# Two query loads and one store moved to ScalarE's DMA queue, and a shorter sum in the last group

## The chip, the cores and the metric

The kernel runs on one core of one Trainium2 chip. A core has five engines that run their own instruction lists in order and wait for each other by semaphores: TensorE (PE; its weight loads are listed as PEld), VectorE (DVE), ScalarE (ACT), GpSimd (POOL) and SyncE (SP). SyncE only issues DMAs here; ScalarE can issue them too, from its own queue. Both queues feed the same 16 DMA engines. In the profile SyncE's row of DMA rings is q1 and ScalarE's is q10. The metric is device microseconds for one execution of the whole program.

## The reference, cut to what matters

The first part is a linear attention with decay. For batch 4, 8 heads, sequence 768 and head size 64, it takes q, k, v and a decay `lam` for each head:

```
intra = (qb @ kb.T * Dmask) @ vb                # inside a block
inter = (qb * lam_pow) @ kv_state               # from earlier blocks
out   = intra + inter
kv_state = lam_block * kv_state + (kb * rev_pow).T @ vb
```

The second part is a feed-forward layer on the 3072 x 512 result: `h = x @ w_in`, `g = h * sigmoid(h)`, output `g @ w_out`, with `w_in` 512 x 2048 and `w_out` 2048 x 512. All inputs and outputs are float32.

## The kernel before, in words

The kernel works on 24 chunks of 128 tokens, all heads at once, in bf16 on TensorE. The feed-forward layer takes the tokens in 12 groups of 256, that is two chunks each. The order on every engine is the order in which the Python code issues the instructions; no scheduler changes it.

**The start.** Line 75 has ScalarE issue the load of `lam` (4 KB, read into 128 partitions). Lines 119 to 131 make the decay tables `lam_fwd` and `lam_bwd` from it, with a table load on ScalarE ahead and another one behind (line 872). The first two pairs of chunks (chunks 0 and 1, chunks 2 and 3) are loaded by the list `LOADS` (line 21), which is walked at line 834 by way of `load_pair` (line 219). A word like `K01` is the letter of the input, the first chunk of the pair (0) and the half of the heads (1). Each word is one DMA of 256 KB, in runs of 512 bytes, and all twelve are issued by SyncE, in the order of the list. In the text Q00 is the query load of the first half of the heads of the first pair, and so on.

What then happens to these tiles is written out by hand in `ORDER` (line 23): `kc` and `qc` scale and cast a half (the first one, `kc:0,0`, is only cast) on VectorE, GpSimd or ScalarE; `tk` and `tq` transpose it on TensorE; `kt` and `qt` copy the transposes out of PSUM; `s` makes the scores, `m` masks them on VectorE, `d` makes the state, `i` and `o` the two parts of the attention, `x` copies the result out, `w` casts a part of `w_in`, `u` and `g` are the first products of the feed-forward layer. `z` puts matmuls on a tile of zeros between them (line 874). On TensorE the start of this list stands as `tk:0,0`, two zero matmuls of 512 columns, `tq:0,0`, four zero matmuls of 256 columns, `tk:0,1`, scores. Weight pieces are loaded by SyncE behind the twelve words, each as soon as a buffer comes free; later pairs of chunks follow them.

Each DMA takes one of eight semaphores in turn (`lam` the first, then the words of the list), and a DMA that uses a semaphore again waits for the one that used it before: Q20 for `lam`, K21 for K00, Q21 for Q00, V20 for K01, V21 for Q01.

**The middle.** Around 35 to 41 us the pair of chunks 4 and 5 is prepared: GpSimd makes eight products (lines 364 and 365) from the loaded queries and keys, TensorE transposes them (lines 399 and 413) between matmuls of the second feed-forward product of the first two groups (line 664).

**The end of a group.** From group 2 on, the product with `w_out` for a group of 256 tokens is done as one step of Strassen's scheme, with seven products instead of eight (`seven`, line 741). `product(g, n, ...)` (line 730) runs product n as eight matmuls into `place[n]` in PSUM. The result is four quarters of 128 tokens by 256 columns in the tile `ob`: quarter 0 is the first tokens and first columns, 1 the first tokens and last columns, 2 and 3 the same for the last tokens. In the last group the seven products come in the order 3, 4, 1, 6, 2, 5, 7, each followed by a small function; product 2 adds into the tile of product 4, and product 5 into that of product 3. The tile `m` holds the sum of products 3, 4 and 1. `last_2` copies quarter 2 out of PSUM on ScalarE and stores it, then makes quarter 3 on VectorE in two steps; `last_5` copies quarter 1 on ScalarE, stores it, and starts quarter 0; `last_7` adds product 7 and stores quarter 0. The four stores of 128 KB each are issued by SyncE (`put`, line 758).

Of the kernel before, what the change touches and what calls it, by code (L numbers as in the profile page):

```python
# [7 lines left out]
F32 = mybir.dt.float32  # L8
BF16 = mybir.dt.bfloat16
AF = mybir.ActivationFunctionType  # L10
AL = mybir.AluOpType

BLK = 128
# [4 lines left out]

NPET = 6

LOADS = "K00 Q00 K01 Q01 V00 V01 K20 Q20 K21 Q21 V20 V21"

ORDER = """
wl kc:0,0,D,u z:24,210 qc:0,0,D tk:0,0,o z:2,512 tq:0,0,att kc:0,1,D,s kt:0,0,A qc:0,1,D z:4 qt:0,0,A tk:0,1,h s:0,0,h,o
# [12 lines left out]
def kernel(  # L37
# [10 lines left out]
    nc = tc.nc  # L48
    B, H, S, D = q.shape
    assert (B, H, S, D) == (4, 8, 768, 64)  # L50
    NB = S // BLK
# [9 lines left out]
    const = ctx.enter_context(tc.tile_pool(name="const", bufs=1))  # L61
# [11 lines left out]
    lam_sb = const.tile([128, H], F32)  # L73
    lam_bc_ap = bass.AP(tensor=lam.tensor, offset=lam.offset, ap=[[0, 128]] + list(lam.ap))
    nc.scalar.dma_start(out=lam_sb, in_=lam_bc_ap)

# [8 lines left out]
        out=ident, in_=ident, compare_op=AL.not_equal, fill=1.0,  # L87
# [4 lines left out]
    for r in range(2):  # L92
        for i in range(2):
            rows = slice(64 * i, 64 * i + 64)
            nc.gpsimd.affine_select(
                out=mask_p[rows, r], in_=mask_p[rows, r], compare_op=AL.is_ge, fill=0.0,
# [5 lines left out]
        out=mask, in_=mask, compare_op=AL.is_ge, fill=0.0,  # L102
# [8 lines left out]
    for i in range(NKV):  # L111
# [14 lines left out]
        op=AL.mult,  # L126
# [11 lines left out]

    wtmp = {}
    pad2 = const.tile([128, 288], mybir.dt.uint8, name="pad2")  # L140

    pairs = [const.tile([128, 2 * H * D], F32, name=f"pair{i}") for i in range(6)]
    npair = iter(range(99))

    def next_pair():
        return pairs[next(npair) % 6]

    def w_piece(which, i, a, b):
        if which == "in":
# [4 lines left out]
    def load_w(which, *pieces):  # L154
        for i in pieces:
            if which == "in" and i > 5:
                tag = "kf" if i == 6 else "vf"
                wtmp[which, i] = []
                for a in range(2):
                    ko, f = w_piece(which, i, a, a + 1)  # L160
                    t = io.tile([128, 1, 512], F32, name=tag, tag=tag, bufs=6)
                    nc.sync.dma_start(out=t, in_=w_in_r[:, ko, f])
                    wtmp[which, i].append(t)
                continue
            ko, f = w_piece(which, i, 0, 2)
            t = next_pair().rearrange("p (k f) -> p k f", k=2)
            nc.sync.dma_start(out=t, in_=(w_in_r if which == "in" else w_out_r)[:, ko, f])
            wtmp[which, i] = t
# [18 lines left out]
    def bank(tag):  # L187
        if tag != "o":
            return {"tag": tag, "bufs": NBUF[tag]}
        otag[0] = 1 - otag[0]  # L190
        return {"tag": f"o{otag[0]}", "bufs": 1}
# [23 lines left out]
    def load_q(c):  # L215

        load_pair(q, c, rawq)

    def load_pair(src, c, dst, parts=((0, H),)):
        b, blk = divmod(c, NB)  # L220
        for lo, hi in parts:
            if c not in dst:
                dst[c] = next_pair().rearrange("p (h r d) -> p h r d", h=H, r=2)
            nc.sync.dma_start(out=dst[c][:, lo:hi].rearrange("p h r d -> p h (r d)"),  # L224
                              in_=src[b, lo:hi, blk * BLK:(blk + 2) * BLK, :].rearrange("h (p r) d -> p h (r d)", r=2))

    rawq, rawk, vraw = {}, {}, {}

    def load_1(src, c, tag, bufs, e=None):
        b, blk = divmod(c, NB)  # L230
# [443 lines left out]
    HALF = DM // 2  # L674
# [25 lines left out]
    lo, hi = slice(0, 128), slice(128, 256)  # L700
# [20 lines left out]
    def g_diff(g, j):  # L721

        one = quad(g, j)
        d = sum_tile(g, "gd", j // 2, 128)[:, j % 2]
        a, b = (hi, lo) if j < 2 else (lo, hi)
        nc.vector.tensor_tensor(d, one[:, :, a], one[:, :, b], op=AL.subtract)  # L726
        for u in range(4):
            gs[g, 6 if j < 2 else 7, 4 * (j % 2) + u] = d[:, u, :]

    def product(g, n, dst, start):  # L730

        tick()
        for k in range(K2):
            if n in (3, 4):
                lhsT = gt[g, k][:, 0:128] if n == 3 else gt[g, K2 + k][:, 128:256]
            else:
                lhsT = gs[g, n, k]
            rhs = w_block(n, k, (0, 0))[:, 0, :] if n == 2 else w_block(n, k, (1, 1))[:, 0, :] if n == 5 else wsum[n, k]
            nc.tensor.matmul(dst, lhsT=lhsT, rhs=rhs, start=(start and k == 0), stop=(k == K2 - 1), skip_group_check=True)  # L739

    def seven(g):

        last = g == len(GROUPS) - 1
        if last:
            tags = ("o0", 1), ("o1", 1), ("att", 3), ("att", 3), ("h", 2)
            tiles = [psum.tile([128, HALF], F32, name="o_last", tag=t, bufs=b, padded_shape=[128, 512]) for t, b in tags]
            place = dict(zip((3, 4, 1, 6, 7), tiles))
            place[5], place[2] = place[3], place[4]
        else:
            o = [psum.tile([128, 2, HALF], F32, name="o_ps", **bank("o")) for _ in range(2)]  # L750
            place = {3: o[0][:, 0, :], 4: o[0][:, 1, :], 5: o[0][:, 0, :], 2: o[0][:, 1, :],
                     1: o[1][:, 0, :], 7: o[1][:, 0, :], 6: o[1][:, 1, :]}
        ob = pairs[g] if g < 6 else opool.tile([128, 4 * HALF], F32, name="ob", tag="ob")
        quarters = ob.rearrange("p (a n) -> p a n", a=4)
        m = work.tile([128, HALF], F32, name="msum", tag="msum", bufs=2)
        r0 = gstart[g]

        def put(rows, cols, src):
            dst = out[r0 + BLK * rows:r0 + BLK * rows + BLK, cols[0]:cols[1]]
            if last:  # L760
                nc.sync.dma_start(out=dst, in_=src)
            elif g < 6:
                held.append((dst, src))
            else:
                stores.append([0, dst, src])

        def after_3():
            nc.scalar.activation(m, place[3], AF.Copy)

        def after_4():  # L770
            if not last:
                after_3()
            nc.vector.tensor_tensor(m, m, place[4], op=AL.add)
            if g > 3:
                g_diff(g, 3)

        def after_sums():
            for j in (2, 3)[g - 2:]:
                g_diff(g, j)

        def after_1():
            nc.vector.tensor_tensor(m, m, place[1], op=AL.add)

        def after_2():
            nc.scalar.activation(quarters[:, 1:3, :], o[0], AF.Copy)
            nc.vector.tensor_tensor(quarters[:, 0::3, :], m[:, None, :].to_broadcast([128, 2, HALF]), o[0], op=AL.subtract)

        def after_7():
            nc.vector.tensor_tensor(quarters[:, 0::3, :], quarters[:, 0::3, :], o[1], op=AL.add)
            for t in range(2):  # L790
                put(t, (0, DM), ob[:, DM * t:DM * t + DM])

        def quarter(a):

            side = (0, 1, 0, 1)[a]
            put(a // 2, (HALF * side, HALF * side + HALF), quarters[:, a, :])

        def last_2():
            nc.scalar.activation(quarters[:, 2, :], place[2], AF.Copy)
            quarter(2)  # L800
            nc.vector.tensor_tensor(quarters[:, 3, :], m, quarters[:, 2, :], op=AL.subtract)
            nc.vector.tensor_tensor(quarters[:, 3, :], quarters[:, 3, :], place[6], op=AL.add)
            quarter(3)

        def last_5():
            nc.scalar.activation(quarters[:, 1, :], place[5], AF.Copy)
            quarter(1)
            nc.vector.tensor_tensor(quarters[:, 0, :], m, quarters[:, 1, :], op=AL.subtract)

        def last_7():  # L810
            nc.vector.tensor_tensor(quarters[:, 0, :], quarters[:, 0, :], place[7], op=AL.add)
            quarter(0)

        if last:
            order = [(3, True, after_3), (4, True, after_4), (1, True, after_1), (6, True, None),
                     (2, False, last_2), (5, False, last_5), (7, True, last_7)]
        else:
            order = [(3, True, None), (4, False, after_4), (1, True, after_sums if g < 4 else None), (6, False, after_1),
                     (5, False, None), (2, False, after_2), (7, True, after_7)]

        def step(n, start, after):
            def run():
                product(g, n, place[n], start)
                if after:
                    after()
            return run

        return [step(*x) for x in order]
# [1 line left out]
    nch = [n // BLK for n in GROUPS]  # L830
    cst = [sum(nch[:g]) for g in range(len(GROUPS))]


    for word in LOADS.split():
        a = int(word[2])
        src, dst = {"Q": (q, rawq), "K": (k, rawk), "V": (v, vraw)}[word[0]]
        load_pair(src, int(word[1]), dst, ((4 * a, 4 * a + 4),))

    later = [("in", i, {f"{t}:{b},{a}" for a in range(2)}) for i, (b, t) in enumerate((b, t) for b in (0, 2) for t in ("kc", "qc", "vc"))]
    later += [("in", 6, set()), ("in", 7, set())] + [("out", i, {f"w:{n},{a}" for a in range(2)}) for n, i in enumerate((0, 1, 4, 5, 2, 3))]  # L840
# [48 lines left out]
    for word in ORDER.split():  # L889
        name, _, args = word.partition(":")  # L890
# [88 lines left out]
    for g in range(2, len(GROUPS) - 1):  # L979
        c, d, a, b = range(2 * g + 2, 2 * g + 6)  # L980
# [79 lines left out]
```

## Time and profile before

| what | us |
|---|---|
| three runs | 196.33, 197.43, 198.35 (median 197.43) |
| the profiled execution | 197.22 |
| its span, from the first to the last instruction | 195.4 |
| TensorE busy | 189.0 |
| VectorE busy | 132.7 |
| ScalarE busy | 101.6 |
| GpSimd busy | 72.7 |

A line of the timeline has the start in us, the duration in us, the engine, the line of the kernel, the operation, what is written and read, and how often it was repeated; brackets give the idle time of the engine before it and what ended that. "SPq" and "ACTq" are the issues of DMAs by SyncE and ScalarE, whose duration is that of the issue and not of the transfer. In the slices each digit is the busy share of one slice in tenths. A queue's line has its packets, its MB, and its time as a share of 16 DMA engines. The trace also records when each of the 16 DMA engines has completed its part of a load; a load has landed when all 16 have. The granted TensorE clock was 0.999 over the span.

### The profile page before, as it was taken

The page shows a single profiled execution, that of the slowest core. Times are in us where ns is not written, and L with a number is a line of the kernel's source. Part 1 is how long each engine was busy: PE and PEld are TensorE (multiplying, and loading weights), DVE is VectorE, ACT ScalarE, POOL GpSimd, SP SyncE. Part 2 cuts the span into 40 slices and gives each one's busy share as a digit, 9 for nine tenths or more (in the row PEclk, how much of TensorE's full clock was granted, in tenths as well). Part 3 has the DMA queues.
Part 4 walks back from the last instruction along what each step waited for, and adds up shares of the span by engine and source line. Part 5 has one row for each costly group of instructions (what it writes and reads, how often), then busy time and mean ns, then how long its engine had stood idle before and what let it go on. Part 6 is the DMA issues. An engine that isn't in the chain of part 4 may idle for free.

```text
span 195.4 us, 6705 instructions
## 1 busy us (share of the span) xinstructions
PE 189.0 (97%) x2859; PEld 154.1 (79%) x2864; DVE 132.7 (68%) x253; ACT 101.6 (52%) x191; POOL 72.7 (37%) x126
## 2 busy tenths in 40 slices
PE   7889999999999999999999999999999999999993
PEld 6568544546888888888888888888888888888882
DVE  1797267978999476875755865975875846754443
ACT  3875974153853844662662652652752752733621
POOL 5240000928937526834704851850940200200000
PEclk9999999999999999999999999999999999999999
DMA  3999999999979799949879499798899840200203
GB/s 93 333 354 406 404 403 334 234 274 280 177 163 285 99 172 245 205 84 229 154 164 236 92 221 158 166 235 168 190 375 220 251 186 3 107 3 0 111 0 107
DMA packets 95581, 38.71 MB, mean 198 GB/s; under 512 B 80960, under 2 KB 88640, under 8 KB 95552
## 3 DMA queue, kind: packets, MB, share of 16 engines
q1 hardware_dynamic: 90208, 36.97, 77.1%
q10 hardware_dynamic: 5344, 1.32, 3.1%
q8 instruction: 22, 0.36, 0.8%
q14 instruction: 7, 0.06, 0.1%
HBM read 27.27 MB, written 6.29 MB: 172 GB/s over the span
## 4 chain that ended last, share of the span: by engine, by line
PE 89%; SPq 3%; DMA 2%; DVE 2%; issue 1%; POOL 1%; ACT 0%; ACTq 0%; DVEq 0%; POOLq 0%
PE h_ps L619 38%; PE o_ps L739 29%; PE o_ps L664 6%; PE h_ps L858 5%; PE op L540 4%; SPq L224 3%; DMA pair<-in_q_dram 2%; PE o_last L739 2%; PE sp L540 2%; PE kv_ps L540 1%; DVE ss L560 1%; POOL vp L253 1%; POOL qb L253 1%; PE op L313 0%; PE op L323 0%
## 5 line engine op out<-in xcount | busy, mean ns | idle before, releaser
L619 PE MATMUL h_ps<-xt,w_in_bf 128*128 128x256 bf16 x672 | 76.2, 272 | 0.0
L619 PEld LDWEIGHTS <-w_in_bf 128*128 128x128 bf16 x672 | 65.4, 98 | 8.9 <-issue 0.3
L631 ACT ACTIVATE g<-h_ps 128x512 bf16<-128x512 f32 x84 | 49.9, 597 | 33.9 <-PE h_ps L619 32.6
L180 POOL CAST kvs<-total 128x256 bf16<-128x256 f32 x26 | 10.4, 407 | 35.8 <-DVE total L575 26.6
L726 DVE TENSOR_TENSOR gd<-g 128x512 bf16<-128x512 bf16 x40 | 20.5, 523 | 3.8 <-ACT g L631 3.8
L364 POOL TENSOR_TENSOR qb<-qf,lam_fwd 128x256 bf16<-128x256 f32 x18 | 12.5, 692 | 20.6 <-DMA qf<-in_q_dram 13.1
L712 DVE TENSOR_TENSOR gc<-g 128x512 bf16<-128x512 bf16 x20 | 10.3, 517 | 14.1 <-ACT g L631 14.1
L178 ACT ACTIVATE xt<-op 128x256 bf16<-128x256 f32 (+1 forms) x18 | 8.1, 484 | 22.5 <-PE op L540 22.5
L739 PE MATMUL o_ps<-w_out_bf,gb 128*128 128x256 bf16 x144 | 18.8, 273 | 0.0
L739 PE MATMUL o_ps<-wsum,gd 128*128 128x256 bf16 x144 | 18.7, 273 | 0.0
L182 DVE CAST xt<-op 128x256 bf16<-128x256 f32 (+1 forms) x16 | 8.3, 541 | 14.9 <-PE op L540 13.9
L739 PE MATMUL o_ps<-wsum,g 128*128 128x256 bf16 x144 | 17.2, 273 | 0.0
L739 PEld LDWEIGHTS <-gd 128*128 128x128 bf16 x160 | 15.7, 98 | 1.8
L739 PEld LDWEIGHTS <-g 128*128 128x128 bf16 x160 | 15.7, 98 | 1.8
L714 DVE TENSOR_TENSOR gb<-g 128x1024 bf16<-128x1024 bf16 x20 | 17.0, 850 | 0.0
L739 PEld LDWEIGHTS <-gb 128*128 128x128 bf16 x160 | 14.9, 98 | 2.0
L364 POOL TENSOR_TENSOR kb<-kf,lam_bwd 128x256 bf16<-128x256 f32 x20 | 14.3, 713 | 5.2 <-DMA kf<-in_k_dram 5.2
L575 DVE TENSOR_TENSOR total<-total,kv_ps 128x256 f32<-128x256 f32 x33 | 13.8, 418 | 2.4 <-ACT total L178 0.2
L664 PE MATMUL o_ps<-w_out_bf,g 128*128 128x512 bf16 x60 | 14.3, 379 | 0.5 <-issue 0.3
L365 POOL TENSOR_TENSOR kb<-kf,lam_bwd 128x256 bf16<-128x256 f32 x20 | 14.3, 714 | 0.0
L365 POOL TENSOR_TENSOR qb<-qf,lam_fwd 128x256 bf16<-128x256 f32 x18 | 13.6, 754 | 0.0
L560 DVE TENSOR_TENSOR ss<-sp,mask 128x512 bf16<-128x512 f32 x20 | 12.8, 681 | 0.2 <-PE sp L540 0.2
(107 smaller groups left out, 251.0 us busy)
## 6 DMA issues: line engine op xcount, KB each, us to landing
vf<-in_v_dram SPq DMA_DIRECT2D x20, 256.0 KB, 4.2
kf<-in_k_dram SPq DMA_DIRECT2D x18, 256.0 KB, 5.0
pair<-in_moe_w_out_dram SPq DMA_DIRECT2D x8, 512.0 KB, 7.8
qf<-in_q_dram SPq DMA_DIRECT2D x15, 256.0 KB, 4.4
pair<-in_moe_w_in_dram SPq DMA_DIRECT2D x6, 512.0 KB, 7.2
out_dram<-pair SPq DMA_DIRECT2D x12, 256.0 KB, 3.8
out_dram<-ob SPq DMA_DIRECT2D x10, 256.0 KB, 3.2
pair<-in_k_dram SPq DMA_DIRECT2D x4, 256.0 KB, 4.5
```

What stands on the lines that cost most here:

```text
L180: nc.gpsimd.tensor_copy(dst, src)
L364: eng.tensor_tensor(dst[:, 0::2], src[:, 0::2, ::-1, :], by[:, 0::2, ::-1, :], op=AL.mult)
L365: eng.tensor_tensor(dst[:, 1::2], src[:, 1::2], by[:, 1::2], op=AL.mult)
L540: ins = nc.tensor.matmul(dst, lhsT=lhsT, rhs=rhs, start=start, stop=True, skip_group_check=True)
L560: nc.vector.tensor_tensor(ss, sp.rearrange("k w p q -> k (w p) q"), mask64[:, None, :].to_broadcast([128, len(scores) * NP, D]), op=AL.mult)
L575: nc.vector.tensor_tensor(total[b], old, place(c, h), op=AL.add)
L619: nc.tensor.matmul(hps[g, i][:, a:a + 256], lhsT=w_in_bf[:, ko, m * 128:(m + 1) * 128], rhs=xt[g][:, ko, :], start=(ko == 0 and u == 0), s ...
L631: nc.scalar.activation(gg.rearrange("p u n -> p (u n)"), hps[g, i], AF.Silu)
L664: nc.tensor.matmul(o, lhsT=gt[g, ko][:, mt * BLK:(mt + 1) * BLK], rhs=w_out_bf[:, ko, :], start=(ko == 0), stop=(ko == KO_OUT - 1))
L714: nc.vector.tensor_tensor(both, low, one, op=AL.add)
L726: nc.vector.tensor_tensor(d, one[:, :, a], one[:, :, b], op=AL.subtract)
L739: nc.tensor.matmul(dst, lhsT=lhsT, rhs=rhs, start=(start and k == 0), stop=(k == K2 - 1), skip_group_check=True)
```

## The change

The words `Q00` and `Q01` of the list become `Q00A` and `Q01A`: ScalarE issues these two loads, behind the load of `lam` and ahead of its first table load. The loop over the list is moved up to directly behind the load of `lam`, with `load_pair` and the buffers that it uses. SyncE issues the other ten words in their order. The semaphores are handed out as before.

In the last group, a new step behind product 6 adds `place[6]` to `m` into quarter 3; behind product 2 only the subtraction of quarter 2 is left to do for quarter 3. Behind product 5, quarter 0 is now started by VectorE straight from PSUM, `m - place[5]`, instead of from the copy that ScalarE made of it; ScalarE's copy of the same tile for quarter 1 comes behind it in the program, and waits for it. The store of quarter 1 is issued by ScalarE.

```diff
-LOADS = "K00 Q00 K01 Q01 V00 V01 K20 Q20 K21 Q21 V20 V21"
+LOADS = "K00 Q00A K01 Q01A V00 V01 K20 Q20 K21 Q21 V20 V21"
...
     nc.scalar.dma_start(out=lam_sb, in_=lam_bc_ap)
+
+    pairs = [const.tile([128, 2 * H * D], F32, name=f"pair{i}") for i in range(6)]
...
+    def load_pair(src, c, dst, parts=((0, H),), e=None):
...
+            (e or nc.sync).dma_start(out=dst[c][:, lo:hi].rearrange("p h r d -> p h (r d)"),
+                              in_=src[b, lo:hi, blk * BLK:(blk + 2) * BLK, :].rearrange("h (p r) d -> p h (r d)", r=2))
+
+    for word in LOADS.split():
+        a = int(word[2])
+        src, dst = {"Q": (q, rawq), "K": (k, rawk), "V": (v, vraw)}[word[0]]
+        load_pair(src, int(word[1]), dst, ((4 * a, 4 * a + 4),), nc.scalar if word[3:] else None)
...
-        def put(rows, cols, src):
+        def put(rows, cols, src, e=None):
             dst = out[r0 + BLK * rows:r0 + BLK * rows + BLK, cols[0]:cols[1]]
             if last:
-                nc.sync.dma_start(out=dst, in_=src)
+                (e or nc.sync).dma_start(out=dst, in_=src)
...
+        def last_6():
+            nc.vector.tensor_tensor(quarters[:, 3, :], m, place[6], op=AL.add)
 
         def last_2():
             nc.scalar.activation(quarters[:, 2, :], place[2], AF.Copy)
             quarter(2)
-            nc.vector.tensor_tensor(quarters[:, 3, :], m, quarters[:, 2, :], op=AL.subtract)
-            nc.vector.tensor_tensor(quarters[:, 3, :], quarters[:, 3, :], place[6], op=AL.add)
+            nc.vector.tensor_tensor(quarters[:, 3, :], quarters[:, 3, :], quarters[:, 2, :], op=AL.subtract)
             quarter(3)
 
         def last_5():
+            nc.vector.tensor_tensor(quarters[:, 0, :], m, place[5], op=AL.subtract)
             nc.scalar.activation(quarters[:, 1, :], place[5], AF.Copy)
-            quarter(1)
-            nc.vector.tensor_tensor(quarters[:, 0, :], m, quarters[:, 1, :], op=AL.subtract)
+            quarter(1, nc.scalar)
...
-            order = [(3, True, after_3), (4, True, after_4), (1, True, after_1), (6, True, None),
+            order = [(3, True, after_3), (4, True, after_4), (1, True, after_1), (6, True, last_6),
                      (2, False, last_2), (5, False, last_5), (7, True, last_7)]
```

More of the change, by code (lines that the diff above doesn't have):

```diff
@@ L75, with next_pair @@
     nc.scalar.dma_start(out=lam_sb, in_=lam_bc_ap)
+    pairs = [const.tile([128, 2 * H * D], F32, name=f"pair{i}") for i in range(6)]
+    npair = iter(range(99))
+    def next_pair():
+        return pairs[next(npair) % 6]
+    rawq, rawk, vraw = {}, {}, {}
+    def load_pair(src, c, dst, parts=((0, H),), e=None):
+        b, blk = divmod(c, NB)
+        for lo, hi in parts:
+            if c not in dst:
+                dst[c] = next_pair().rearrange("p (h r d) -> p h r d", h=H, r=2)
+            (e or nc.sync).dma_start(out=dst[c][:, lo:hi].rearrange("p h r d -> p h (r d)"),
[4 more added lines that the diff above has]
+        load_pair(src, int(word[1]), dst, ((4 * a, 4 * a + 4),), nc.scalar if word[3:] else None)
     pad = const.tile([128, PAD], mybir.dt.uint8, name="pad")
@@ L140 @@
     pad2 = const.tile([128, 288], mybir.dt.uint8, name="pad2")
[L142 to L146, printed above, removed]
     def w_piece(which, i, a, b):
@@ L217, in load_q @@
         load_pair(q, c, rawq)
[L219 to L227, printed above, removed]
     def load_1(src, c, tag, bufs, e=None):
@@ L791, in after_7, with quarter @@
                 put(t, (0, DM), ob[:, DM * t:DM * t + DM])
-        def quarter(a):
+        def quarter(a, e=None):
             side = (0, 1, 0, 1)[a]
-            put(a // 2, (HALF * side, HALF * side + HALF), quarters[:, a, :])
+            put(a // 2, (HALF * side, HALF * side + HALF), quarters[:, a, :], e)
+        def last_6():
+            nc.vector.tensor_tensor(quarters[:, 3, :], m, place[6], op=AL.add)
         def last_2():
@@ L831 @@
     cst = [sum(nch[:g]) for g in range(len(GROUPS))]
[L834 to L837, printed above, removed]
     later = [("in", i, {f"{t}:{b},{a}" for a in range(2)}) for i, (b, t) in enumerate((b, t) for b in (0, 2) for t in ("kc", "qc", "vc"))]
```

## The prediction

> **What bounds the kernel now.** I read the page's totals first, then the slices, the chain of work that ended last, and the timelines of the first 17 us, of 36 to 41 us and of the last 5 us.
>
> ```profile
> span 195.4 us, 6705 instructions
> ...
> PE 189.0 (97%) x2859; PEld 154.1 (79%) x2864; DVE 132.7 (68%) x253; ACT 101.6 (52%) x191; POOL 72.7 (37%) x126
> ...
> DMA  3999999999979799949879499798899840200203
> ```
>
> TensorE is busy for 97% of the span, and DMA is full from slice 1 to about slice 10. So there are two candidates for the bound early on, and only TensorE later. The window of 0 to 16 us of the DMA view (0.4 us a digit) and that of 2.5 to 4 us place the start of the saturation:
>
> ```profile
> DMA  0000001597899999999999999999999999999999
> ```
>
> ```profile
> q1 hardware_dynamic: 434, 0.22, 62.0%
> ```
>
> SyncE's row q1 moves 0.22 MB at 62% of 16 engines between 2.5 and 4.0 us; from 4.0 us on everything is at 9. What comes after 4.0 us is ordered by bytes, not by issue time. The issues, and the first two users on VectorE, in the timeline:
>
> ```profile
> 0.80 0.45 SPq L224 DMA_DIRECT2D pair<-in_k_dram  x1
> ...
> 1.32 0.48 SPq L224 DMA_DIRECT2D pair<-in_q_dram  x1
> ...
> 1.85 0.50 SPq L224 DMA_DIRECT2D pair<-in_k_dram  x1
> ...
> 2.39 0.51 SPq L224 DMA_DIRECT2D pair<-in_q_dram  x1
> ...
> 2.94 2.35 SPq L224 DMA_DIRECT2D pair<-in_v_dram  x2
> ...
> 5.26 0.43 DVE L182 CAST kp<-pair 128x512 bf16<-128x512 f32 x1 [0.39 <-DMA pair<-in_k_dram]
> ...
> 6.08 0.69 DVE L253 TENSOR_TENSOR qb<-pair,lam_fwd 128x512 bf16<-128x512 f32 x1 [0.39 <-DMA pair<-in_q_dram]
> ```
>
> Four issues go out in 0.5 us each; the next two (V00, V01) take 2.35 us together, because the queue is full by then. The trace's landing record has K00, Q00, K01, Q01, V00, V01, K20, Q20 complete at 5.24, 5.98, 6.79, 7.55, 8.28, 9.02, 9.84 and 10.58: one 256 KB load per 0.74 us, on every one of the 16 engines from its first load on (the first engine finishes K00 at 3.70 and Q00 at 4.46). No engine has a gap between K00 and Q00 for an earlier issue to fill. The chain goes on as follows:
>
> ```profile
> 6.07 4.51 DMA pair<-in_q_dram
> 10.65 1.04 POOL qb L253
> ...
> 16.68 3.60 PE h_ps L619 x32
> ```
>
> The stage hangs on Q20's landing, the eighth load, and on TensorE's first feed-forward matmul at 16.68. A second anchor stands at 37 to 41 us:
>
> ```profile
> 37.58 0.39 PEld L399 LDWEIGHTS <-qb 128*128 128x128 bf16 x7 [0.32 <-POOL qb L365]
> ...
> 39.07 0.81 PE L664 MATMUL o_ps<-w_out_bf,g 128*128 128x512 bf16 x3
> ...
> 39.94 0.39 PE L413 MATMUL tk<-ident,kb 128*128 128x128 bf16 x4
> ```
>
> There TensorE waits for GpSimd, whose eight products run back to back from 34.62, when the DMA of the query pair lands. The tail:
>
> ```profile
> 191.36 0.38 ACT L806 ACTIVATE ob<-o_last 128x256 f32<-128x256 f32 x1 [0.49 <-PE o_last L739]
> ...
> 191.78 0.42 DVE L808 TENSOR_TENSOR ob<-msum,ob 128x256 f32<-128x256 f32 x1
> ...
> 192.31 0.42 DVE L811 TENSOR_TENSOR ob<-ob,o_last 128x256 f32<-128x256 f32 x1
> ```
>
> The last store is issued at 192.78, right behind the last sum (192.73), and lands at 194.55; the span ends 0.85 later.
>
> **The change, part by part.**
>
> *Issue times at the start.* On ScalarE Q00 goes out behind the lam load (0.80 plus 0.42), at about 1.27 instead of 1.32, and Q01 at about 1.8 instead of 2.39. On SyncE K01 moves from 1.85 to about 1.32 and V00 from 2.94 to about 1.85. The order on SyncE behind them is unchanged, as is everything that it waits for. Since each engine is busy from its first descriptor on, I take 0 for the earlier issue. The end on the good side: if all the idle share of 2.5 to 4.0 us were filled (38% of 1.5 us), 0.57 us.
>
> *ScalarE's own queue.* Two issues of about 0.5 us push its table load (1.25, 1.28 us long) to about 2.3 and its end to 3.6. The next instruction waits for lam, landed at 4.35 and used at 4.38. So 0 while that cover of 0.75 us stands; without it, third rival. The moved queries share semaphores with Q21 and V21, which SyncE issues at 7.50 and 9.20; Q00 and Q01 landed at 5.98 and 7.55 before, so 1.5 us cover them.
>
> *Sharing of the engines.* This is the cost. K00 had the engines to itself; now Q00 is in a second row beside it, and K01 beside Q01. The two loads of a pair need 1.48 us of each engine in either order, so the later of the pair lands where Q did (5.98, 7.55), and the K at worst there too: K00 from 5.24 to 5.98, +0.74; at best unchanged. What that does: the cast of K00 (0.43) would run 6.00 to 6.43, its four transposes start at 6.48 instead of 5.74, the two 512-column zero matmuls that are ordered behind them (0.86) end at 7.74 instead of 7.00, and the transposes of Q00 start 0.74 later. From there TensorE, ScalarE and VectorE hand over in lockstep; VectorE is busy without a break from 9.27 to 14.40 and waits only 0.18 (at 14.59, for V21, which does not move). So up to 0.56 reaches the last score product of the stage (now ending at 16.21) and the first feed-forward matmul. Bounds 0 and 0.56. The nearest row, queue 10 starting beside a backlog in q1, is the window of 44.5 to 45.0: q10 has 505 packets and q1 has 50; from 45.25 to 46.5 it is 490 against 839. A fresh row gets at least its share, so I take a value at the upper end, 0.5.
>
> The Trainium skill (DMA: Bandwidth & Descriptors, Queues, rings and completion order) says that each DMA engine goes round between the rows it has work for, a packet at a time. By that rule K00 and Q00 end together, and this term would be 0.56; by the half microsecond at 44.5, Q00 would even come first. No run here shows two rows filling in the first microseconds.
>
> *What 37 to 41 us gives back.* The eight transposes at 37.38 take 0.61 where 0.44 is their pace (four take 0.22 at 38.85), a wait of 0.17; the three matmuls from 39.07 end at 39.72 at 216 ns each and the next transposes start at 39.94, a wait of 0.22. Both end on GpSimd work that is tied to a landing, hence to bytes. A TensorE that arrives up to 0.39 late loses nothing: 0.5 becomes 0.1. By the same rows, a start that is earlier while the bytes are not would be given back too.
>
> *The tail.* Removed: a subtraction (0.43) for quarter 3 that waited for ScalarE. Added: a sum m + place[6] (0.42) right after product 6, in VectorE's idle time from 189.16 to 190.90; the subtraction after it starts at 190.90 as before, so quarter 3 is stored at about 191.38 instead of 191.88. Quarter 0's subtraction reads PSUM and starts with product 5's end at about 191.36, not 191.78. The compiled order shows ScalarE's copy of that tile now waiting for it: from about 191.82 to 192.20 instead of 191.36 to 191.74. Only its store is queued behind it on ScalarE; it goes out at about 192.25, where SyncE's went at 192.31. The last sum waited for VectorE's own result (192.20 plus 0.10); now it waits for product 7 alone, which ends at 192.20 too. Other hand-overs from TensorE took 0.04, so it starts at about 192.24: -0.07. Bounds: 0 and -0.11. SyncE was free at 192.69 for the last store already; losing one issue brings nothing.
>
> *Sum.* The profiled execution took 197.22 (span 195.4 and 1.8 around it): 197.22 + 0.10 - 0.07 = 197.25. It stands 0.21 under the median of the three runs (196.33, 197.43, 198.35), so the forecast as a median is 197.4 to 197.5, written 197.4: no change.
>
> **The rivals.**
> *The start is filled.* Two rows fill the engines sooner, the whole byte stream and with it the anchor at 34.62 come 0.57 earlier. For it: 62% between 2.5 and 4.0. Against it: K00 to Q00 takes 0.76 on the first engine, so none idled between loads. 197.43 - 0.57 - 0.07 = 196.8.
> *Slower, nothing absorbed.* The pair K00/Q00 lands together and the delay of 0.56 at 16.68 reaches the end, since the waits at 37 to 41 us move along with it. It decides once the first feed-forward matmul starts over 0.39 later than 16.68 and GpSimd's 34.62 moves too. Against it: 34.62 is released by a DMA. 197.43 + 0.56 - 0.07 = 197.9; with the whole 0.74 it is 198.1.
> *ScalarE blocks at its issue.* SyncE's fifth load took 1.61 to issue and ended at 4.56. If the limit is common to both rows, Q01 is caught, the table load ends at 5.84 and log_lam runs at 5.87 instead of 4.38: 1.49 late, less 0.18 and 0.39 is 0.92, and 198.3. Against it: at 42.41 and 42.92 ScalarE issued in 0.42 and 0.54 while SyncE stood in issues of 0.97 and 1.34.
> *The ScalarE store ends last.* It has until 194.48, 2.2 us after its issue. The stores now land in 1.7; the lam load on that row took 3.55. With that it lands at 195.80, 1.25 after today's last: 198.7.
>
> **How the numbers follow.** Forecast 0.52, filled start 0.20, nothing absorbed 0.16, ScalarE blocked 0.07, late store 0.05. Runs of one kernel differ by 1.0 to either side of their median, which widens each case. From 196.5 to 198.4 holds about 8 in 10: it takes in 196.8 and 198.1 and leaves the last two cases partly out. One per cent is 2.0 us, about what a measurement of this kernel can tell from no change; no single case reaches it, so faster by over 1% gets 0.04, slower 0.06, within 0.90.
>
> **What would show it.** K00's cast at 5.7 to 6.0 instead of 5.26, and the first feed-forward matmul at 17.0 to 17.2, show the sharing; a cast at 5.26 or before refutes it. GpSimd's first product at 34.62 within 0.2, and shorter waits at 37.4 and 39.9, show the anchor. log_lam at 4.38 shows ScalarE free. The last sum 0.04 after product 7 shows the tail. The prediction is wrong if 34.62 moves, or if ScalarE's store is the last to land.

## The result, and the profile after

The changed kernel took 199.5 us (median of six runs, 199.11 to 200.88) against 197.79 us of the kernel before in the same session (six runs, 196.33 to 198.35): a ratio of 1.0105, 95% interval 1.0058 to 1.0151. (Here and below the ratio is an estimate from the single runs and not the quotient of the two medians; two slow runs, one each of `after_same_addr` and `start_same_addr`, are left out of it.) It is slower by about 1%, and the forecast of 197.4 with its range to 198.4 was wrong. The profiled execution of after took 199.11 us, with a span of 197.3; the one of before took 197.22, with 195.4.

The page of after, its totals, slices and the shares of the chain of work that ended last:

```profile
span 197.3 us, 6704 instructions
...
PE 188.4 (95%) x2859; PEld 153.2 (78%) x2864; DVE 132.9 (67%) x253; ACT 101.8 (52%) x191; POOL 72.6 (37%) x126
...
DMA  3999999999959878988979699999699980200203
GB/s 83 304 299 385 393 399 361 218 286 248 240 107 278 152 164 174 225 160 184 203 92 268 116 162 215 103 220 242 129 334 317 150 307 3 76 35 0 110 0 106
...
PE 77%; DMA 16%; DVE 2%; POOL 1%; SPq 1%; issue 1%; ACT 0%; ACTq 0%; POOLq 0%
```

The same two rows on the page of before, which the prediction did not show:

```profile
GB/s 93 333 354 406 404 403 334 234 274 280 177 163 285 99 172 245 205 84 229 154 164 236 92 221 158 166 235 168 190 375 220 251 186 3 107 3 0 111 0 107
...
PE 89%; SPq 3%; DMA 2%; DVE 2%; issue 1%; POOL 1%; ACT 0%; ACTq 0%; DVEq 0%; POOLq 0%
```

TensorE is busy no longer than before (188.4 against 189.0), so the 1.9 us are waits. In the chain DMA has gone from 2% to 16%. In the row of digits DMA is at 9 in the early slices of both kernels. Only the row of GB/s tells them apart: in the slices 1 and 2 (about 5 to 15 us) it falls from 333 and 354 to 304 and 299. The 16 engines are as busy as before, and move less.

The DMA view of the window from 8.5 to 11.5 us, in which only loads of keys, queries and values run; first before, then after:

```profile
DMA packets 2050, 1.02 MB, mean 339 GB/s; under 512 B 63, under 2 KB 2050, under 8 KB 2050
```

```profile
DMA packets 1752, 0.87 MB, mean 290 GB/s; under 512 B 53, under 2 KB 1752, under 8 KB 1752
```

It is the same kind of work, packets of 512 bytes, and 15% fewer of them in the same 3 us. In the trace the mean packet of this window takes 26.7 ns before and 33.4 ns after. The landing record (the last of the 16 engines, us):

| | K00 | Q00 | K20 | Q20 | K21 | Q21 | V21 | 1st weights | 4th weights |
|---|---|---|---|---|---|---|---|---|---|
| before | 5.24 | 5.98 | 9.84 | 10.58 | 11.32 | 12.05 | 14.56 | 15.83 | 19.56 |
| after | 5.40 | 6.51 | 10.75 | 11.64 | 12.54 | 13.46 | 16.32 | 17.68 | 21.73 |

From K20 to Q21 a load takes 0.74 us before and 0.90 after (three loads, 2.21 and 2.71 us). V21 is 1.76 late: K00 has 0.16 of that already, and the eleven loads behind it add 1.60, somewhat less than eleven times 0.16. A weight piece of 512 KB takes 1.24 before and 1.35 after, and the fourth is 2.17 late.

What hangs on these bytes, first two rows of the timeline of before:

```profile
16.61 3.12 PE L619 MATMUL h_ps<-xt,w_in_bf 128*128 128x256 bf16 x27
...
34.62 0.74 POOL L364 TENSOR_TENSOR qb<-pair,lam_fwd 128x256 bf16<-128x256 f32 x1 [20.51 <-DMA pair<-in_q_dram]
```

then the timeline of after:

```profile
1.25 1.01 ACTq L90 DMA_DIRECT2D pair<-in_q_dram  x2
...
2.30 1.28 ACT L141 ACT_TABLE_LOAD   x1 [2.30 <-issue]
...
2.96 1.67 SPq L90 DMA_DIRECT2D pair<-in_k_dram  x1
...
4.58 0.21 ACT L142 ACTIVATE log_lam<-lam_sb 128x8 f32<-128x8 f32 x1 [1.00 <-DMA lam_sb<-in_lam_dram]
...
5.42 0.43 DVE L198 CAST kp<-pair 128x512 bf16<-128x512 f32 x1 [0.34 <-DMA pair<-in_k_dram]
...
6.61 0.69 DVE L260 TENSOR_TENSOR qb<-pair,lam_fwd 128x512 bf16<-128x512 f32 x1 [0.76 <-DMA pair<-in_q_dram]
...
17.76 0.63 ACT L194 ACTIVATE w_in_bf<-pair 128x512 bf16<-128x512 f32 x1 [0.32 <-DMA pair<-in_moe_w_in_dram]
...
18.45 1.27 PE L626 MATMUL h_ps<-xt,w_in_bf 128*128 128x256 bf16 x10
...
42.20 0.39 PE L420 MATMUL tk<-ident,kb 128*128 128x128 bf16 x4
```

and in its chain of work, which before went through TensorE here:

```profile
12.22 8.15 DMA pair<-in_moe_w_in_dram
20.45 7.84 DMA pair<-in_moe_w_out_dram
28.31 0.70 DVE w_out_bf L198
29.03 7.80 DMA pair<-in_q_dram
37.08 0.99 POOL qb L371
```

The first casts are only 0.16 and 0.53 late. The first feed-forward matmul is at 18.45 instead of 16.61 (in the timeline of before; 16.68 in its chain), since it waits for a part of `w_in` that waits for its landing. Three loads in a row lead to GpSimd's first product at 37.08 instead of 34.62. From there the delay goes down only a little: the transposes of line 420 are at 42.20 instead of 39.94, the first product of the last group starts at 187.97 instead of 185.92, which is 2.05. The last sum ends the story in the timeline of after:

```profile
192.96 0.43 DVE L811 TENSOR_TENSOR ob<-ob 128x256 f32<-128x256 f32 x1 [0.87 <-ACT ob L809]
193.11 0.86 PEld L746 LDWEIGHTS <-gd 128*128 128x128 bf16 x8
193.21 1.04 PE L746 MATMUL o_last<-wsum,gd 128*128 128x256 bf16 x8
193.41 0.42 DVE L815 TENSOR_TENSOR ob<-msum,o_last 128x256 f32<-128x256 f32 x1
193.87 0.38 ACT L816 ACTIVATE ob<-o_last 128x256 f32<-128x256 f32 x1 [0.95 <-DVE ob L815]
194.28 0.37 ACTq L768 DMA_DIRECT2D out_dram<-ob  x1
194.29 0.42 DVE L820 TENSOR_TENSOR ob<-ob,o_last 128x256 f32<-128x256 f32 x1 [0.45 <-PE o_last L746]
```

Product 7 ends at 194.25 and the sum of line 820 starts 0.04 later, as against 0.105 before: the 0.07 that the prediction gave the tail. ScalarE's store lands at 196.00, the last one of SyncE at 196.43.

### The profile page after: what moved, and what is told of

Its sections match the earlier page's. It is cut to its first block, busy times and chain, and to the rows that moved or that the text cites. A ratio compares the mean times of both kernels' runs of the same rounds, so it can differ in the third digit from the quotient of the medians.

```text
span 197.3 us, 6704 instructions
## 1 busy us (share of the span) xinstructions
PE 188.4 (95%) x2859; PEld 153.2 (78%) x2864; DVE 132.9 (67%) x253; ACT 101.8 (52%) x191; POOL 72.6 (37%) x126
## 4 chain that ended last, share of the span: by engine, by line
PE 77%; DMA 16%; DVE 2%; POOL 1%; SPq 1%; issue 1%; ACT 0%; ACTq 0%; POOLq 0%
PE h_ps L626 36%; PE o_ps L746 28%; DMA pair<-in_moe_w_in_dram 4%; DMA pair<-in_moe_w_out_dram 4%; DMA pair<-in_q_dram 4%; DMA pair<-in_v_dram 4%; PE op L547 4%; PE o_last L746 3%; PE o_ps L671 3%; PE sp L547 2%; PE kv_ps L547 1%; POOL qb L371 1%; SPq L90 1%; DVE ss L567 1%; POOL qb L372 1%; SPq L183 1%
## 5 line engine op out<-in xcount | busy, mean ns | idle before, releaser
L733 DVE TENSOR_TENSOR gd<-g 128x512 bf16<-128x512 bf16 x40 | 21.5, 548 | 4.0 <-ACT g L638 4.0
L721 DVE TENSOR_TENSOR gb<-g 128x1024 bf16<-128x1024 bf16 x20 | 16.4, 818 | 0.0
```

The lines of the kernel that those rows point to most:

```text
L721: nc.vector.tensor_tensor(both, low, one, op=AL.add)
```

## The experiments

Every ratio is to the kernel before, run on the same chip in the same session (medians of before in the three sessions: 197.05, 197.44 and 197.36 us).

**First session: which part?** My first theory after the result was the second row of DMA rings at the start: with q10 beside q1 each engine changes between rows, and that makes each packet dearer. It makes the start alone slow, and a kernel without it as quick as before. The rivals were the tail, and a profile out of the ordinary. Both kernels were also run once more, unchanged.

> The kernel before, unchanged, for a second trace. If the stream of loads is slowed by the change (theory), the loads from V00 to V20 land 0.74 to 0.75 us apart as in the first trace, V21 lands near 14.6 and GpSimd's first product of chunks 4 and 5 starts near 34.6. If the rate of the stream is a matter of the single execution (rival), 0.90 us apart can be seen here too.

> The changed kernel, unchanged, for a second trace. Theory: again 0.90 us from load to load between V01 and V20, V21 near 16.3, GpSimd's first product near 37.1, time 199 to 200. Rival (chance of the single execution): 0.74 us apart, and a time near 197.5.

Measured: 196.91 and 199.78 us. A load from K20 to Q21 takes 0.74 and 0.90 us again, and GpSimd's first product starts at 34.75 and 36.98. Both rates belong to the kernels, not to one execution.

`start_only` is after with the last group of before:

```diff
-        def last_6():
-            nc.vector.tensor_tensor(quarters[:, 3, :], m, place[6], op=AL.add)
...
-            nc.vector.tensor_tensor(quarters[:, 0, :], m, place[5], op=AL.subtract)
...
-            quarter(1, nc.scalar)
+            quarter(1)
```

> Only Q00 and Q01 on ScalarE, the end as before. Theory (the loss comes from the loads): slower by 1.8 to 2.2 us, ratio 1.009 to 1.011, with loads 0.90 us apart. Rival (the loss comes from the end): within 0.3 us of before.

`tail_only` is after with the twelve loads back on SyncE, in the order of before; the loop and the buffers stay where the change has put them:

```diff
-LOADS = "K00 Q00A K01 Q01A V00 V01 K20 Q20 K21 Q21 V20 V21"
+LOADS = "K00 Q00 K01 Q01 V00 V01 K20 Q20 K21 Q21 V20 V21"
```

> Only the change of the last group; SyncE issues all twelve loads in the old order. Theory: faster by 0.1 to 0.2 us (last sum 0.07 earlier after product 7, last store landing 0.08 sooner), ratio 0.999 to 1.000, loads 0.74 us apart. Rival (ScalarE's copy that now waits for VectorE, or its store, is late): slower by 1 us or more.

Measured: `start_only` 199.53 us, 1.0117 (1.0087 to 1.0147; expected up to 1.011), 0.90 us per load. `tail_only` 199.51 us, 1.0120 (1.0090 to 1.0149), 0.89 us per load, GpSimd at 36.99. So a kernel in which SyncE issues the same loads in the same order as before is as slow as after. The theory of the two rows fell with it. The tail is no better a culprit, since `start_only` has the old one. What the two slow kernels share with after, and not with before, is the block that moved up, and the line in it that gives tiles another place: `pairs = [...]`, the six buffers into which all these loads go, now stands directly behind `lam_sb`. Tiles of this pool lie behind each other in each partition in the order in which the program makes them. In the compiled programs the first buffer starts at byte 22528 before, behind all tables and a pad of 288 bytes, and at byte 16544 after (16512, where `lam_sb` starts, plus its 32 bytes). 22528 is 88 times 256; 16544 is 64 times 256 and 160 over. Every buffer has 4096 bytes and every row 512, so all rows of all six share that remainder.

**Second session: the address.** Theory: where the buffers start sets the rate of the loads. Rivals: the queues or the new last group after all, each alone. `before_moved` is the kernel before with that one line moved, and nothing else:

```diff
     nc.scalar.dma_start(out=lam_sb, in_=lam_bc_ap)
+    pairs = [const.tile([128, 2 * H * D], F32, name=f"pair{i}") for i in range(6)]
...
-    pairs = [const.tile([128, 2 * H * D], F32, name=f"pair{i}") for i in range(6)]
```

> The kernel before with one edit: the six load buffers are allocated directly behind lam, as in the changed kernel, so they start at byte 16544 of each partition (32 past a multiple of 128) instead of 22528 (a multiple of 512). Every engine's order is that of before. Theory A (the address of the buffers slows the loads into them): loads 0.88 to 0.91 us apart, GpSimd's first product near 37, ratio 1.010 to 1.013. Theory B (the loads are slow because two queues fill the engines, and the run with only the new tail was slow for a reason of its own): loads 0.74 to 0.75 apart, ratio 0.998 to 1.002.

`after_same_addr` is the whole change with the tables and pads allocated ahead of `pairs`, in their old order, so that every tile lies where it did before; `start_same_addr` is that with the old last group; `tail_same_addr` is before with the new last group alone.

```diff
+    NKV = 3
+    pad = const.tile([128, PAD], mybir.dt.uint8, name="pad")
+    iota_i = const.tile([128, 2 * NB], mybir.dt.int32)
...
+    pad2 = const.tile([128, 288], mybir.dt.uint8, name="pad2")
     pairs = [const.tile([128, 2 * H * D], F32, name=f"pair{i}") for i in range(6)]
```

> The changed kernel in its own order on every engine, with every buffer at the address it had before (22528). Theory A: loads 0.74 to 0.75 us apart, GpSimd's first product within 0.3 us of 34.6, ratio 0.997 to 1.002. Theory B: as slow as the changed kernel, ratio 1.010 to 1.013.

> Only Q00 and Q01 on ScalarE, all buffers at their old addresses. Theory A: the two queues alone cost or bring little; the first matmul of the feed-forward layer at 16.6 to 17.2, of which up to 0.4 is given back at 37 to 41 us, ratio 0.998 to 1.003. Theory B: 1.010 to 1.013.

> Only the new last group, all buffers at their old addresses, the list of loads where it was. Both theories of the start: loads 0.74 to 0.75 us apart. The tail alone: last sum 0.07 earlier behind product 7 and the last store 0.08 shorter, so 0.1 to 0.2 us faster, ratio 0.999 to 1.000. Rival (the tail itself costs, and made the run with the new tail slow): ratio over 1.005.

Measured, with the time per load again from K20 to Q21:

| kernel | us per load | GpSimd's first product, us | median, us | ratio and interval |
|---|---|---|---|---|
| `before_moved` | 0.91 | 37.58 | 199.35 | 1.0090 (1.0055 to 1.0126) |
| `after_same_addr` | 0.74 | 34.80 | 197.23 | 1.0005 (0.9978 to 1.0032) |
| `start_same_addr` | 0.74 | 35.16 | 197.56 | 1.0003 (0.9977 to 1.0028) |
| `tail_same_addr` | 0.74 | 35.20 | 197.21 | 0.9981 (0.9956 to 1.0006) |

One moved line makes the kernel before as slow as after, without any of the new issues or the new tail. All of the change without the moved line can't be told from before (0.9978 to 1.0032, that is from 0.4 us less to 0.6 us more). The theory of the address holds, and the queues and the tail are worth nothing that these runs can tell from zero. Two ratios lie just under what was expected, 1.0090 under 1.010 and 0.9981 under 0.999, with intervals that reach into it. In the profile of `before_moved` K00 landed at 6.01, 0.77 later than in before; that is part of its 37.58, but not of its time per load. The moved line also shifts the tables behind the buffers, which the next session shows not to be needed for the loss.

**Third session: which multiple?** The kernel before once more, with a few bytes taken from the pad ahead of the six buffers and put behind them, so that nothing else moves:

```diff
-    pad2 = const.tile([128, 288], mybir.dt.uint8, name="pad2")
+    pad2 = const.tile([128, 32], mybir.dt.uint8, name="pad2")
...
+    pad3 = const.tile([128, 256], mybir.dt.uint8, name="pad3")
```

This is `shift_256`. In `shift_128`, `shift_64` and `shift_32` 128, 64 and 32 bytes are moved in the same way. The starts are 22272, 22400, 22464 and 22496. The text on `shift_128` has a slip: its "384 bytes in all" should be 128, from 22528 to 22400.

> The kernel before with only the six load buffers moved down by 256 bytes of each partition: the first starts at byte 22272, a multiple of 256 but not of 512. If the rate needs starts at multiples of 256 (the Trainium skill, DMA: Bandwidth & Descriptors, on how a descriptor splits into transactions, speaks of 256), or of less, a load of keys or queries lands every 0.74 to 0.75 us, GpSimd starts its first product of chunks 4 and 5 at 34.6 to 35.2 us, and the ratio is 0.998 to 1.002. If it needs multiples of 512 (the size of one row of these loads): about 0.90 us per load, GpSimd at 36.9 to 37.6, ratio 1.009 to 1.013.

> The same, moved down by 384 bytes in all: the first buffer starts at byte 22400, a multiple of 128 but not of 256. If a multiple of 256 is what counts: 0.85 to 0.92 us per load, GpSimd at 36.5 to 37.6, ratio 1.007 to 1.013. If 128 or less is enough: 0.74 to 0.75, 34.6 to 35.2, 0.998 to 1.002.

> The first buffer starts at byte 22464, a multiple of 64 but not of 128. If a multiple of 128 or 256 is what counts: 0.85 to 0.92 us per load, GpSimd at 36.5 to 37.6, ratio 1.007 to 1.013. If 64 is enough: 0.74 to 0.75, 34.6 to 35.2, 0.998 to 1.002.

> The first buffer starts at byte 22496, a multiple of 32 but not of 64, as in the changed kernel (16544), but with every other buffer where the kernel before has it. By the theory of the address: about 0.90 us per load, GpSimd at 36.9 to 37.6, ratio 1.009 to 1.013, whatever the multiple that counts. If instead the distance from some other buffer counts, and not the start itself: 0.74 to 0.75, 34.6 to 35.2, 0.998 to 1.002, and the theory of the address falls.

| kernel | start modulo 256 | us per load | GpSimd's first product, us | median, us | ratio and interval |
|---|---|---|---|---|---|
| `shift_256` | 0 | 0.76 | 34.5 | 197.41 | 0.9989 (0.9958 to 1.0019) |
| `shift_128` | 128 | 0.88 | 36.8 | 199.06 | 1.0104 (1.0021 to 1.0186) |
| `shift_64` | 192 | 0.90 | 37.1 | 199.25 | 1.0093 (1.0058 to 1.0128) |
| `shift_32` | 224 | 0.91 | 37.3 | 200.39 | 1.0146 (1.0110 to 1.0183) |

The window from 8.5 to 11.5 us in the DMA view of `shift_256`, and in that of `shift_128`:

```profile
DMA packets 2087, 1.04 MB, mean 346 GB/s; under 512 B 62, under 2 KB 2087, under 8 KB 2087
```

```profile
DMA packets 1743, 0.87 MB, mean 289 GB/s; under 512 B 51, under 2 KB 1743, under 8 KB 1743
```

and GpSimd's first products of the query pair in the view by tile, with their first and last start, for the same two kernels:

```profile
L365 POOL TENSOR_TENSOR qb<-pair,lam_fwd x2: 612/634/657, 34.5 to 36.1; 128x256 bf16<-128x256 f32 x2
```

```profile
L365 POOL TENSOR_TENSOR qb<-pair,lam_fwd x2: 608/840/1073, 36.8 to 38.4; 128x256 bf16<-128x256 f32 x2
```

256 is enough: 22272 is not a multiple of 512, and its loads run as before. 128 is not enough. The 0.76 of `shift_256` lies a hundredth over what was expected, because its K20 landed early (9.73 against 9.84); its Q21 landed at 12.02, before at 12.05; its GpSimd was a tenth earlier than expected (34.48). How far off the boundary the row starts makes no difference to the rate: 1743, 1751 and 1754 packets in this window for 128, 192 and 224, and 1752 for the 160 of after. `shift_32` has the highest ratio, over the 1.013 that was expected; in its profile `lam` landed 0.7 us later than in before, and its interval overlaps those of the other two; whether 224 is dearer than 128 stays open.

## Why the prediction was wrong, step by step

**The step that failed** is the price of a load in "What bounds the kernel now": "one 256 KB load per 0.74 us, on every one of the 16 engines". I took it as a constant of the chip, and with "what comes after 4.0 us is ordered by bytes, not by issue time" I concluded that no edit of the issues could move the bytes. The second sentence is right and turned against the forecast: if the bytes order everything, their price is the first thing to look at. It was 0.90. The edit that changed it is in the diff (`+    pairs = [...]`), and my account of the change has no term for it; it costed the issues that the loop makes and not the tiles that moved up with it. The term of the sum that was missing is about 0.15 us for each of the eleven loads behind K00, and V21 is 1.76 late; with the weight pieces it has grown to 2.17 at the fourth of them and to 2.46 at GpSimd's first product, and 2.05 of it is left in the last group. Less 0.07 at the last sum and 0.08 for the last store (1.69 us from issue to landing, 1.77 before) that is the 1.9 by which the span grew; the medians differ by 1.7.

The Trainium skill (DMA: Bandwidth & Descriptors, How a descriptor splits into AXI transactions) says that a descriptor, here one row, is cut into transactions of 256 bytes that have to start at a 256-byte boundary, and that where the row starts off it the first one begins at the boundary below and costs additional beats of 32 bytes. It speaks of bytes that are read, while here the side in SBUF moved, which is written. This rule of the Trainium skill spoke against the change and was not weighed. The runs agree with its boundary: shifts of 0 and 256 bytes are quick, 32, 64 and 128 are not. An estimate from the count of the Trainium skill is 20, 22 and 23 beats instead of 16 for a row of 512 bytes that starts 128, 192 or 224 over, that is 25 to 44% more. The runs have 0.88 to 0.91 us against 0.74, about 20% more for each of the three. So the boundary is that of the Trainium skill and the size is not, and the measurement decides.

**Earlier issues at the start: 0.** Right. With the old addresses, 0.47 MB had moved between 2.5 and 5.0 us, against 0.49 before, the sixth load (V01) landed at 8.99 instead of 9.02, and the first weight piece at 16.17 instead of 15.83. "The start is filled" is refuted.

**ScalarE's queue: 0.** Right. Its two issues took 1.01 us, the table load started at 2.30, and `log_lam` at 4.58 waited only for `lam`, landed at 4.56. That is 0.2 later than 4.38, because `lam` itself was (4.35 before), and Q00's product waited for its load all the same. "ScalarE blocks at its issue" is refuted: SyncE's fifth issue took 1.67 us (1.61 before), while ScalarE's two beside it took 0.46 and 0.53. The slow issue came again as the fifth of SyncE's own, although it is the seventh of the loads in after.

**Sharing of the engines: 0.5.** Too much, and hidden by the larger error. It can be read in `after_same_addr`, where the rate is the old one. In the DMA view from 2.5 to 5.0 us:

```profile
q1 hardware_dynamic: 607, 0.30, 42.7%
q10 hardware_dynamic: 426, 0.17, 27.9%
```

and in its timeline:

```profile
5.24 0.43 DVE L197 CAST kp<-pair 128x512 bf16<-128x512 f32 x1 [0.23 <-DMA pair<-in_k_dram]
6.33 0.69 DVE L259 TENSOR_TENSOR qb<-pair,lam_fwd 128x512 bf16<-128x512 f32 x1 [0.66 <-DMA pair<-in_q_dram]
```

Two rows do share the engines, but the row that started later got the smaller share here (0.17 of 0.47 MB; some 107 of its packets are those of `lam`, as before). K00's cast is at 5.24 (5.26 before), and Q00's product is 0.25 late (6.08 before). That K00 and Q00 would land together, as the prediction worked out from the rule of the Trainium skill (DMA: Bandwidth & Descriptors, Queues, rings and completion order), was not seen: they landed at 5.22 and 6.23. The row of 44.5 us, by which I chose the upper end, had a backlog on the other side and was no model for two rows that both begin; and the window behind it, with 490 packets against 839, had already less than half for the fresh row. The first feed-forward matmul started at 16.94, 0.33 after that of before; `tail_same_addr`, without any sharing, had it at 17.02, so these 0.33 can't be put down to sharing.

**What 37 to 41 us gives back: 0.39.** Too much: of the two waits only the first, 0.17, exists. The second, 0.22, was read from "the three matmuls from 39.07", but the timeline of before has four weight loads for them:

```profile
39.02 0.59 PEld L664 LDWEIGHTS <-g 128*128 128x128 bf16 x4
```

So the record of one matmul is missing from the trace. Four at 216 ns take 0.86, and the transposes start 0.87 behind 39.07: nothing waited. In `after_same_addr`, where all four records are there, the same stretch goes from 39.24 to 40.11, 0.87 again. The first wait did what the prediction said of it. In `after_same_addr` GpSimd started at 34.80, within 0.2 of 34.62, and TensorE came 0.33 late to the eight transposes and left them 0.17 late (37.38 and 37.99 before):

```profile
37.71 0.61 PE L405 MATMUL tq<-ident,qb 128*128 128x128 bf16 x8
...
38.16 1.03 PE L670 MATMUL o_ps<-w_out_bf,g 128*128 128x512 bf16 x4
```

There the wait is used up, and 0.17 is still there at 40.11 (39.94 before). With 0.17 instead of 0.39 the prediction's own 0.10 would have been 0.33, still far from 1.7. (`tail_same_addr`, whose start is that of before, had GpSimd at 35.20, so executions alone can move this mark by 0.6.) In after the anchor itself moved by 2.46. TensorE waited for GpSimd's products until 39.85, and that wait handed the delay on instead of taking it up: "the prediction is wrong if 34.62 moves" came true, by a mechanism that none of the rivals had. "Nothing absorbed" named the same two marks (over 0.39 late at the first feed-forward matmul, and 34.62 moving), but its cause and its size, 0.56, were not those measured.

**The tail: -0.07.** The mechanism is shown in the trace of after (0.04 behind product 7 instead of 0.105) and its ScalarE store was not the last to land. In the runs `tail_same_addr` has 0.9981, which is -0.37 us with an interval from -0.87 to +0.12: too wide to tell 0.07 from nothing.

## What to carry to other kernels

When a diff moves an allocation, work out where each buffer starts before and after it, and look at the remainder modulo 256 of everything that a DMA fills: here one moved line cost 1% of the kernel, while the rest of the diff cost and gained nothing that can be measured. A row of busy digits at 9 did not tell here what the DMA engines get done (339 or 290 GB/s), so compare GB/s, or packets in a fixed window, next to it. And when an experiment that puts back "the change" stays slow, list what it still shares with the slow kernel in place, not only in order.

## What the runs showed of the hardware that was not expected

A load from HBM whose rows of 512 bytes start at a multiple of 256 bytes in the partition ran at 0.74 to 0.76 us per 256 KB in all six profiles of that kind (two of before, the three with the old addresses, `shift_256`), and at 0.88 to 0.91 in all eight others. The cost seems to be one per row, not per byte: 0.16 us over the 32 rows that each of the 16 engines has in a 256 KB load are 5 ns a row, and 0.11 us over the 16 rows of 2 KB in a 512 KB weight piece are 7 ns. That is worked out from two row lengths only, and no run here tried a third.

Two DMA rows that fill at the start did not slow the sum: the sixth load landed at 8.99 and 9.14 us in `after_same_addr` and `start_same_addr`, and at 8.98 to 9.16 in the four profiles with one row and the same alignment. From 5.0 to 7.5 us, where both rows were busy, the mean packet of 512 bytes took 27.0 to 27.6 ns in either row, and 27.0 to 27.5 ns with one row.
